# Linear attention with a token-mixing MLP on one core: W_tok loaded and transposed first, its row sums as extra columns, k^T v of two batches in 64x64 tiles

## Chip, core and metric

One core of a Trainium2 chip runs one launch. The metric is the device time of that launch in microseconds. The engines are TensorE (PE), VectorE (DVE), ScalarE (ACT), GpSimd (POOL) and the sync engine SP; SP and POOL issue the DMAs.

## What is computed

Eight batches, eight heads, 576 tokens, head width 64, so 512 features; all inputs and the output are float32.

```python
kv  = einsum('bhsd,bhse->bhde', k, v)
out = einsum('bhsd,bhde->bhse', q, kv)
x   = out / sqrt(mean(out * out, -1) + 1e-6) * g_norm      # heads side by side: (8, 576, 512)
a1  = alpha1 * x + beta1
u   = x + lam * einsum('ts,bsd->btd', w_tok, a1)           # w_tok is 576 x 576
a2  = alpha2 * u + beta2
y   = u + lam * (maximum(a2 @ w_ch1, 0) @ w_ch2)           # 512 -> 2048 -> 512
```

## The kernel before

The program is a list of operations. Each has an engine, operands and a cost that the author set; `schedule` (a planner that runs when the kernel is built) turns the list into one fixed order for each engine and for the DMA issues of SP and POOL. At run time every engine goes through its order and waits at semaphores. PE's operations are in two lists: `main` holds the FFN, `ch1` (L1002, a2 @ w_ch1, 16 groups of 4 matmuls of 512 columns), `ch1_tail` (L1014) and `ch2` (L1031); `fill` holds the rest, which the planner weaves between matmuls of `main`. Where PE would have nothing in the head, fillers are put in (`idler`, matmuls of a tile of ones, L597). `P.shift` and `P.gate` are tables by operation number: the first moves an operation's place in the order, the second lets a DMA wait for another operation.

A batch goes through these steps. `kv` (L749, L755) makes k^T v from k and v as they lie in `kr` and `vr`: rows of 4 tokens, 1024 bytes, by `load_kv` (L1186) and the last 64 tokens apart (L1190); 16 matmuls of 128x128 and 4 for the tail. q is brought to `qt`, transposed: in batches 2 to 7 by DVE (`qt_steady`, L1196, L1199) from rows of 128 bytes (`load_q`, L1178), in batches 0 and 1 by PE (`qt_early`, L703), after a copy on POOL (L698). `norm` (L843, 5 chunks of 4 matmuls) makes q times kv, and ACT (square L807, root L813) and DVE (L810 to L825) the normalized x in `xm` and, times the row e1 = alpha1 * lam * 8 * g_norm, `rm`. `tok` (L914) and `tok_tail` (L948) multiply with the transposed W_tok in `wt`; x is added by DVE (L921). `a2_dma` makes a2 on POOL (L986, L989) and transposes it by DMA (L993) to `a2m`, from which `ch1` starts. `finish` (L1058, L1063) multiplies with lam, adds u, and the output goes out.

Batches 0 and 1 are special. Batch 0's q, k and v come as twelve pieces of two heads each (four of q, of k and of v; 128 partitions with rows of 9 tokens, 2304 bytes; `load_pair`, L611), and its steps are done in halves of four heads: `kv_first` (L725) takes 64x64 matmuls, two row tiles in turn (heads 2p and 2p+1), first for one pair and then for the next; `norm_half` (L864) and `tok_half` (L929) make the norm and the token mix of half the features, with products on POOL (L831, L833), and `a2_pair` (L968, L972) transposes a2 on PE. The row e1 and g are made from four small loads on one partition (L655 to L664) and spread to 128 partitions by a matmul with a row of ones (`e1_rows`, L678, L681).

W_tok (576 x 576) is needed transposed, in bf16, and beta1 is put into the token mix as an extra row of the contraction: `wt`'s last block holds 64 token rows and, at the partitions 64 and 96 for even batches, the sums over s of W_tok, split in a bf16 part and the rest. `rtl`'s rows there hold lam * beta1 (L671). Before, W_tok is loaded after batch 0's q, k and v (L629, one DMA of 1152 KB, and L631), 25 transposes (L1081, L1084) go into `wt` by ACT (L1087, L1092), and `wsums` makes the sums from the finished `wt`: ten matmuls with a matrix `pick` (L1103, L1105), two copies on ACT (L1110) and two subtractions on DVE (L1113). A copy for odd batches follows by DMA (L1118).

The loads of batch 1 are `load_kv(1)` on POOL's queue, after batch 0's last v, and its q on SP's, as pieces of two heads; W1 (L1163) and W2 (L1169) come on POOL's queue in three and two DMAs, converted from float32.

Of the kernel before, what the change touches and what calls it, by code (L numbers as in the profile page):

```python
# [14 lines left out]
NB = 8  # L15
# [38 lines left out]
class Prog:  # L54
    ENGINES = ("PE", "ACT", "DVE", "POOL")

    def __init__(self, nc, stack):
        self.nc, self.stack = nc, stack
        self.ops, self.lastw, self.readers = [], {}, {}
        self.ps = stack.enter_context(nc.psum_tensor("ps", [128, 8, 512], F32))  # L60
        self.eng = {"PE": nc.tensor, "ACT": nc.scalar, "DVE": nc.vector,
                    "POOL": nc.gpsimd, "SP": nc.sync}
        self.spares = 0
        self.pools = {"main": (0, 1, 2, 3), "fill": (4, 5, 6, 7), "any": tuple(range(1, 8))}
        self.main, self.fill = [], []
# [4 lines left out]
        self.gate = {}  # L70

# [36 lines left out]
    def op(self, q, cost, fn, r=(), w=(), pri=0.0, lat=0.15, after=()):  # L108
        o = Op(q, "c", cost, lat, [fn], self.bias + pri, len(self.ops))
        o.bias = self.bias  # L110
        return self._add(o, r, w, after)
# [8 lines left out]
    def mm(self, stream, cols, fns, r=(), w=(), slow=False, after=(), margin=0.3,  # L120
# [8 lines left out]
        o.bias = self.bias  # L129
        o.margin, o.narrow, o.urgent = 0.0 if urgent else margin, cols < 512, urgent  # L130
# [4 lines left out]
    def schedule(self):  # L135
# [26 lines left out]
        for o in self.ops:  # L162
# [4 lines left out]
            elif o.pri - o.bias > -900:  # L167
                o.pri = 1e4 + o.pri
        self.fill.sort(key=lambda o: o.pri)
# [10 lines left out]
        rings = {e: deque() for e in ("SP", "POOL", "ACT")}  # L180
        t, left = 0.0, len(self.ops)
# [38 lines left out]
        def take(o, t, cost=None):  # L220
# [7 lines left out]
            if o.kind == "d":  # L228
                rings[o.q].append([o, t + (1.9 if o.q == "POOL" else 1.1), o.nbytes, False, o.ns,
# [59 lines left out]
        while left:  # L289
# [3 lines left out]
            while moved:  # L293
# [17 lines left out]
                if free["PE"] <= t + 1e-9:  # L311
# [20 lines left out]
                    elif f is not None:  # L332
# [4 lines left out]
                        if f.kind == "w" and not self.began:  # L337
                            g = [o for o in fill[:self.reach] if o.kind == "m" and can(o, t)]
                            if g:
# [3 lines left out]
                                f.end = t + c + f.lat  # L343
# [84 lines left out]
    def woven(f, m):  # L428
# [3 lines left out]
        while i < n or j < k:  # L432
            if i < n and (j >= k or i * k <= j * n):
# [67 lines left out]
def bass_transnormer_attn__then__resmlp_affine_kernel(  # L501
# [15 lines left out]
    with ExitStack() as stack:  # L517
# [6 lines left out]
        pick = sb("pick", [128, 128], BF16)  # L524
# [39 lines left out]
        def nine(flat):  # L564
# [3 lines left out]
        sv = nine(qs[:, 0:2304])  # L568
        hf = hh[:].bitcast(F32)
        wl = hf[:, 0:2304].rearrange("p (c s) -> p c s", c=4)  # L570
        wlt = hf[0:64, 2304:2880]
        qi = [[x.rearrange("p (c f) -> p c f", c=9) for x in y] for y in (
            (hf[:, 2880:4032], tmp[:].rearrange("p i f -> p (i f)")[:, 0:1152]),
# [21 lines left out]
        P.bias = -1000.0  # L595
# [10 lines left out]
        lo, up = slice(0, 64), slice(64, 128)  # L606

        def load_pair(b, n, x, dst, p, after=()):


            P.dma("SP", "%s%d_%d" % (n, b, p), dcost(128, 92), lambda e: e.dma_start(  # L611
# [4 lines left out]
        def load_half(p):  # L616
            for n, x, dst, pp in (("q", q, q0s, (p, p + 1)), ("k", k, k0s, (p,)),
                                  ("v", v, sv, (p,)), ("k", k, k0s, (p + 1,)),
                                  ("v", v, sv, (p + 1,))):
                for i in pp:  # L620
                    load_pair(0, n, x, dst, i)

        load_half(0)
        for i, x, n in ((0, moe_alpha1, DM), (1, moe_lam, DM), (4, g_norm, DH),
                        (2, moe_beta1, DM)):
            P.dma("SP", "row%d" % i, 0.17, lambda e, i=i, x=x, n=n: e.dma_start(
                rows[0:1, i, 0:n], x[None, :]), w=[("row", i)], issue=0.5)
        load_half(2)
        P.dma("SP", "wl", dcost(512, 92), lambda e: e.dma_start(  # L629
            wl, moe_w_tok[0:512, :].rearrange("(c p) s -> p c s", p=128)), w=["wl"])  # L630
        P.dma("SP", "wlt", dcost(64, 220), lambda e: e.dma_start(  # L631
            wlt, moe_w_tok[512:576, :]), w=["wlt"])
        for i, x in enumerate((moe_alpha2, moe_beta2)):
            P.dma("SP", "cst%d" % i, 0.17, lambda e, i=i, x=x: e.dma_start(
# [8 lines left out]
        P.op("DVE", dve(64), lambda e: e.memset(pick[:], 0.0), w=["pick"])  # L643
        P.op("DVE", dve(4), lambda e: e.memset(pick[:, 0:128:32], 1.0), r=["pick"], w=["pick"])
# [9 lines left out]
        P.bias = -500.0  # L654
        y = P.op("DVE", 0.67, lambda e: e.tensor_tensor(  # L655
            out=row(0), in0=row(0), in1=row(1), op=ALU.mult), r=[("row", 0), ("row", 1)],
            w=[("row", 0)])
        x = P.op("DVE", 0.67, lambda e: e.tensor_tensor(
            out=lbrow, in0=row(2), in1=row(1), op=ALU.mult), r=[("row", 1), ("row", 2)],
            w=[("row", 3)])  # L660
        P.op("DVE", 0.2, lambda e: e.tensor_scalar(
            out=row(1, DH), in0=row(4, DH), scalar1=8.0, scalar2=None, op0=ALU.mult),
            r=[("row", 4)], w=[("row", 1)], after=[x, y])
        P.op("DVE", 0.67, lambda e: e.tensor_tensor(  # L664
# [3 lines left out]
            r=[("row", 1), ("row", 0)], w=[("row", 0)])  # L668
        for i, h in ((0, 64), (1, 0)):
# [23 lines left out]
        def qt_early(b, j):  # L693
# [7 lines left out]
            for i in range(3):  # L701
# [4 lines left out]
                    r=["ident", ("qi", b, j, 0), ("qi", b, j, 1)], w=[t], slow=True, urgent=True)  # L706
# [12 lines left out]
        def kv_first(j):  # L719


            ts = [P.bank("any") for _ in range(2)]
            for m in range(2):
                p = 2 * j + m
                P.mm("fill", 64, [lambda e, c=c, s=s, t=t, m=m, p=p: e.matmul(  # L725
                    t.ap(slice(64 * m, 64 * m + 64))[:, 0:64],
                    k0s[64 * s:64 * s + 64, p, c, :], sv[64 * s:64 * s + 64, p, c, :],
                    start=(c == 0), stop=(c == 8), tile_position=(64 * s, 64 * m))
                    for c in range(9) for s, t in enumerate(ts)],
                    r=[("st", "k", p), ("st", "v", p)], w=ts, slow=0.09, urgent=True)  # L730
            for s, t in enumerate(ts):
                for m, rs in enumerate((lo, up)):
                    dst, src = kvc[rs, 0, 2 * j + s, 64 * m:64 * m + 64], lambda t=t, rs=rs: t.ap(
                        rs)[:, 0:64]
                    if s:
                        P.op("DVE", dve(64), lambda e, dst=dst, src=src: e.tensor_copy(
                            out=dst, in_=src()), r=[t], w=[("kv%d" % m, 0, 2 * j + s)], pri=-20)
                    else:
                        P.op("ACT", act(64), lambda e, dst=dst, src=src: e.activation(
                            dst, src(), ACT.Identity), r=[t], w=[("kv%d" % m, 0, 2 * j + s)],  # L740
# [52 lines left out]
        def norm_ops(rs, n, t, xks, rks, dest, shape, flat=None, by="DVE"):  # L793
# [24 lines left out]
            if flat is None:  # L818
# [15 lines left out]
                out=x, in0=x, in1=gv, op=ALU.mult), r=xks + ["g"], w=xks)  # L834
# [19 lines left out]
        def norm_half(j, ch):  # L854
# [18 lines left out]
            if ch == 2:  # L873
# [22 lines left out]
                     "DVE" if j else "POOL")  # L896
# [8 lines left out]
        def wk(b, sc):  # L905
            return [("wt", sc), ("wtt", sc)] if sc < 4 else [("wt", tw(b)), ("wtt", 4), ("ws", tw(b))]
# [69 lines left out]
        def a2_dma(b, c):  # L976
# [3 lines left out]
            else:  # L980
# [5 lines left out]
            P.op("POOL", pool(512), lambda e: e.tensor_tensor(  # L986
# [5 lines left out]
            landing[b] = [P.dma(  # L992
                "SP", "t%d" % c, 0.7, lambda e: e.dma_start_transpose(dst, a2b[:, c]),  # L993
                r=[("a2b", c)], w=dk, issue=0.6)]

# [79 lines left out]
        wtt = P.bank("any")  # L1075

        def wt_group(sc):
            t = P.bank("any")
            n = 128 if sc < 4 else 64
            cols = slice(128 * sc, 128 * sc + n)  # L1080
            P.mm("fill", 128, [lambda e, tc=tc: e.transpose(  # L1081
                t.ap(slice(0, n))[:, 128 * tc:128 * tc + 128], wl[:, tc, cols], ident[:])
                for tc in range(4)], r=["ident", "wl"], w=[t], slow=True)
            P.mm("fill", 64, [lambda e: e.transpose(  # L1084
                wtt.ap(slice(0, n))[:, 64 * sc:64 * sc + 64], wlt[:, cols], ident[0:64, 0:64])],
                r=["ident", "wlt"], w=[wtt], slow=True)
            P.op("ACT", act(512), lambda e: e.activation(  # L1087
                wt[0:n, sc, 0:512], t.ap(slice(0, n)), ACT.Identity), r=[t], w=[("wt", sc)])

        def wt_tail():  # L1090
            for a, z, n in ((0, 4, 128), (4, 5, 64)):
                P.op("ACT", act(64 * (z - a)), lambda e, a=a, z=z, n=n: e.activation(  # L1092
                    wt[0:n, a:z, 512:576],
                    wtt.ap(slice(0, n))[:, 64 * a:64 * z].rearrange("p (c t) -> p c t", t=64),
                    ACT.Identity), r=[wtt], w=[("wtt", i) for i in range(a, z)])

        def wsums():


            for a, z in ((0, 512), (512, 576)):  # L1100
                t = P.bank("any")
                n = z - a
                P.mm("fill", n, [lambda e, sc=sc, t=t, a=a, z=z, n=n: e.matmul(  # L1103
                    t.ap()[:, 0:n], pick[:, :], wt[:, sc, a:z], start=(sc == 0), stop=False)
                    for sc in range(4)] + [lambda e, t=t, a=a, z=z, n=n: e.matmul(  # L1105
                        t.ap()[:, 0:n], pick[0:64, :], wt[0:64, 4, a:z], start=False,
                        stop=True)],
                    r=["pick"] + [(k, i) for k in ("wt", "wtt") for i in range(5)], w=[t])
                for i, h in ((4, 64),):
                    P.op("ACT", act(n), lambda e, i=i, h=h, t=t, a=a, z=z, n=n: e.activation(  # L1110
                        wt[h:h + 64, i, a:z], t.ap(slice(h, h + 64))[:, 0:n], ACT.Identity),
                        r=[t, ("ws", i)], w=[("ws", i)])
                    P.op("DVE", dve(n), lambda e, i=i, h=h, t=t, a=a, z=z, n=n: e.tensor_tensor(  # L1113
                        out=wt[h + 32:h + 64, i, a:z],
                        in0=t.ap(slice(h + 32, h + 64))[:, 0:n], in1=wt[h + 32:h + 64, i, a:z],
                        op=ALU.subtract), r=[t, ("ws", i)], w=[("ws", i)])
            for a, z, key in ((0, 64, ("ws", 5)), (64, 0, ("wt", 5))):
                P.dma("SP", "wt%d" % z, (0.3, 70.0), lambda e, a=a, z=z: e.dma_start(  # L1118
                    wt[a:a + 64, 5, :], wt[z:z + 64, 4, :]), r=[("wt", 4), ("wtt", 4), ("ws", 4)],
                    w=[key])  # L1120

        gate = ()
        for j in range(2):
# [210 lines left out]
```

## Time and profile before

| | |
|---|---|
| time, median of 3 runs | 355.2 us (354.76 to 356.05) |
| profiled execution | 356.56 us, of which 354.8 us are its span |
| PE busy in the span | 341.3 us (96%), 2208 matmul records |
| DVE, ACT, POOL busy | 189.8, 149.0, 161.4 us |
| W_tok's load, issue to landing | 8.3 us |
| first token mix of batch 0 (L929) | 36.54 us |
| first FFN matmul (L1002) | 44.37 us |
| DMA | 48.76 MB, mean 137 GB/s |

The profile is one execution; its times count from the start of the span. Busy time of an engine doesn't tell whether its work was useful: PE's 341.3 us hold 20.0 us of fillers (L597). A line of a group reads: line, engine, operation, output<-input, shapes, count, busy us, mean ns of one, idle us of the engine just before them and what ended it. A float32 matmul that isn't of the kind fp32r appears as two records where it takes two passes.

### The profile page before, as it was taken

How to read it: one execution, taken by the hardware profiler on the slowest of the kernel's cores; microseconds unless marked ns; L12 is line 12 of the kernel's file. 1: busy time of each engine (PE TensorE's matmuls, PEld its weight loads, DVE VectorE, ACT ScalarE, POOL GpSimd, SP SyncE). 2: the span in 40 equal slices, each digit the busy share in tenths (PEclk: the TensorE clock that was granted, in tenths of full speed). 3: DMA queues.
4: the chain of work that ended last, by engine and by line, in shares of the span. 5: the costliest groups of instructions: out<-in, count | busy, mean ns of one | idle time of the engine just before them, and what ended most of it. 6: DMA issues, size and time to landing. Idle time of an engine off the chain costs nothing.

```text
span 354.8 us, 5512 instructions
## 1 busy us (share of the span) xinstructions
PE 341.3 (96%) x2208; PEld 198.4 (56%) x2241; DVE 189.8 (54%) x343; ACT 149.0 (42%) x291; POOL 161.4 (45%) x151
## 2 busy tenths in 40 slices
PE   4979999999999999999999999999999999999994
PEld 3858964454664664466556545564476444444644
DVE  3475778204685579636745676459444963210043
ACT  3335397004940386126823366136552273026400
POOL 2397410965308940985058612973192306930000
PEclk9989999999999999999999999999999999999999
DMA  7999899969598399138963995239922110330012
GB/s 241 267 336 161 139 251 230 144 110 198 120 262 134 90 232 213 31 93 195 247 61 76 221 173 124 46 116 258 175 33 89 59 31 15 75 105 0 2 69 79
DMA packets 107952, 48.76 MB, mean 137 GB/s; under 512 B 81997, under 2 KB 99925, under 8 KB 107928
## 3 DMA queue, kind: packets, MB, share of 16 engines
q1 hardware_dynamic: 82312, 27.71, 42.9%
q0 software_dynamic: 25616, 20.71, 34.0%
q8 instruction: 17, 0.28, 0.3%
q14 instruction: 7, 0.06, 0.1%
HBM read 38.82 MB, written 9.44 MB: 136 GB/s over the span
## 4 chain that ended last, share of the span: by engine, by line
PE 87%; DMA 5%; SPq 2%; POOL 2%; DVE 1%; issue 1%; ACT 0%; DVEq 0%; POOLq 0%
PE ps L1031 31%; PE ps L1002 31%; PE ps L914 8%; PE ps L1014 4%; PE ps L843 3%; DMA hh<-in_moe_w_tok_dram 2%; PE ps L749 2%; DMA w<-in_k_dram 2%; PE ps L597 1%; SPq L611 1%; PE ps L929 1%; POOL a1f L986 1%; PE ps L948 1%; PE ps L1081 1%; PE ps L1042 1%; DMA lam_bc<-in_moe_lam_dram 1%
## 5 line engine op out<-in xcount | busy, mean ns | idle before, releaser
L1031 PE MATMUL ps<-w,hh 128*128 128x512 bf16 x543 | 135.3, 383 | 0.7 <-issue 0.3
L1002 PE MATMUL ps<-a2m,w 128*128 128x512 bf16 x501 | 117.8, 381 | 1.0 <-DVE tmp L1058 0.4
L997 ACT ACTIVATE hh<-ps 128x512 bf16<-128x512 f32 x144 | 84.8, 597 | 64.3 <-PE ps L1002 54.9
L1031 PEld LDWEIGHTS ps<-w,hh 128*128 128x128 bf16 x560 | 52.9, 97 | 58.8 <-issue 1.6
L1002 PEld LDWEIGHTS ps<-a2m,w 128*128 128x128 bf16 x512 | 48.7, 98 | 56.5 <-DVE tmp L1058 1.3
L986 POOL TENSOR_TENSOR a1f<-xm,a_bc 128x512 f32<-128x512 f32 x28 | 35.5, 1273 | 68.6 <-DVE xm L921 68.3
L1058 DVE TENSOR_TENSOR tmp<-ps,lam_bc 128x512 f32<-128x512 f32 (+2 forms) x38 | 25.1, 661 | 69.8 <-PE ps L1031 56.5
L1063 POOL TENSOR_TENSOR xm<-xm,tmp 128x512 f32<-128x512 f32 x28 | 35.4, 1269 | 34.7 <-DVE tmp L1058 34.7
L810 DVE TENSOR_REDUCE small<-sq 128x8 f32<-128x512 f32 (+2 forms) x41 | 27.2, 666 | 25.2 <-ACT sq L807 25.0
L989 POOL TENSOR_TENSOR a2b<-a1f,b_bc 128x512 bf16<-128x512 f32 x32 | 40.3, 1273 | 0.7
L843 PE MATMUL ps<-kvc,qt 128*128 128x128 f32 x140 | 40.1, 395 | 0.0
L921 DVE TENSOR_TENSOR xm<-ps,xm 128x512 f32<-128x512 f32 x28 | 19.3, 690 | 29.8 <-PE ps L914 28.5
L749 PE MATMUL ps<-vr,kr 128*128 128x128 f32 x112 | 32.3, 395 | 0.0
L807 ACT ACTIVATE sq<-ps 128x512 f32<-128x512 f32 (+2 forms) x41 | 23.9, 584 | 19.3 <-PE ps L843 18.5
L1199 ACT ACTIVATE qt<-qp 128x576 fp32r<-128x576 f32 x24 | 15.9, 682 | 32.3 <-DVE qp L1196 32.3
L843 PEld LDWEIGHTS ps<-kvc,qt 128*128 128x128 f32 x140 | 27.4, 199 | 2.0
L914 PE MATMUL ps<-rm,wt 128*128 128x512 bf16 x109 | 28.3, 379 | 0.2
L597 PE MATMUL ps<-fil 128*128 128x128 bf16 x109 | 20.0, 245 | 4.5 <-DVE fil L596 4.5
L819 DVE TENSOR_TENSOR ps<-ps,small 128x512 f32<-128x512 f32 (+1 forms) x35 | 23.5, 690 | 0.5
L766 ACT ACTIVATE kvo<-ps 64x256 f32<-64x256 f32 x14 | 5.3, 378 | 43.0 <-PE ps L755 42.8
L749 PEld LDWEIGHTS ps<-vr,kr 128*128 128x128 f32 x112 | 22.3, 201 | 0.9
L1196 DVE STREAM_TRANSPOSE qp<-qs 128x576 f32<-128x576 f32 x24 | 17.3, 755 | 5.6 <-DMA qs<-in_q_dram 3.4
(109 smaller groups left out, 324.0 us busy)
## 6 DMA issues: line engine op xcount, KB each, us to landing
out_dram<-xm SPq DMA_DIRECT2D x32, 256.0 KB, 2.3
kr<-in_k_dram POOLq DMA_DIRECT2D x7, 1024.0 KB, 9.0
vr<-in_v_dram POOLq DMA_DIRECT2D x7, 1024.0 KB, 11.4
qs<-in_q_dram SPq DMA_DIRECT2D x24, 288.0 KB, 11.1
w<-in_moe_w_ch_dram POOLq DMA_DIRECT2D x3, 1024.0 KB, 10.2
xm<-in_q_dram SPq DMA_DIRECT2D x8, 288.0 KB, 4.4
w<-in_k_dram SPq DMA_DIRECT2D x4, 288.0 KB, 5.6
qs<-in_v_dram SPq DMA_DIRECT2D x4, 288.0 KB, 5.9
```

The lines of the kernel that those rows point to most:

```text
L749: P.mm("fill", 128, [lambda e, t=t, c=c, h=h, o=128 * (h % 4): e.matmul(t.ap()[:, o:o + 128], kr4[:, h, c:c + 2, :].rearrange("p c d -> p ...
L807: P.op("ACT", act(n), lambda e: e.activation(sq[rs, s3, 0:nst, :].rearrange("p h e -> p (h e)"), ps(), ACT.Square), r=[t], w=[("sq", s3)])
L810: P.op("DVE", dve(n), lambda e: e.tensor_reduce(out=st, in_=sq[rs, s3, 0:nst, :], axis=AX.X, op=ALU.add), r=[("sq", s3)], w=[("sm", s4)])
L843: P.mm("fill", 128, [lambda e, p=p: e.matmul(dst(p), qt[:, p, cs], kvc[:, i, p, :], start=(p == 0), stop=(p == 3)) for p in range(4)], r=[ ...
L914: P.mm("fill", 512, [lambda e, sc=sc: e.matmul(t.ap(), wt[:, sc if sc < 4 else tw(b), 128 * c:128 * c + 128], rsrc(b, sc, al), start=(sc = ...
L986: P.op("POOL", pool(512), lambda e: e.tensor_tensor(out=a1f[:, s], in0=x, in1=a2_bc[:], op=ALU.mult), r=ks + ["a2"], w=[("a1f", s)])
L989: P.op("POOL", pool(512), lambda e: e.tensor_tensor(out=a2b[:, c], in0=a1f[:, s], in1=b2_bc[:], op=ALU.add), r=[("a1f", s), "b2"], w=[("a2 ...
L997: P.op("ACT", act(512), lambda e: e.activation(dst, t.ap(), ACT.Relu), r=[t], w=keys, pri=-1000)
L1002: P.mm("main", 512, [lambda e, dj=dj: e.matmul(t.ap(), w1[:, dj, 128 * fj:128 * fj + 128], a2m[:, b % 3, dj, :], start=(dj == 0), stop=(dj ...
L1031: P.mm("main", 512, [lambda e, fj=fj, t=t, c=c: e.matmul(t.ap(), (ht[:, fj, 128 * c:128 * c + 128] if c < 4 else hl[:, fj, :]), w2[:, fj, ...
L1058: P.op("DVE", dve(z - a), lambda e: e.tensor_tensor(out=tmp[:, s, a:z], in0=t.ap()[:, 0:z - a], in1=lam_bc[:, a:z], op=ALU.mult), r=[t, "l ...
L1063: lambda e: e.tensor_tensor(out=x, in0=x, in1=tmp[:, s, a:z], op=ALU.add),
```

## The change

W_tok is loaded first: five DMAs of 128 (the last 64) rows, ahead of batch 0's q, k and v. Each is transposed when it lands, four transposes to a group. W_tok's tile has 64 more columns, set to zero by POOL; DVE sums each row (`tensor_reduce`), writes the sum's bf16 value into column 576 and the rest into column 608, and the last 128 columns, with the sums among them, are transposed as the fifth block. `pick` and `wsums` are gone, and the copy for the odd batches stays.

`kv_first` takes two pairs in one group: four 64x64 tiles in turn (two row tiles, two column tiles). It is also used for batch 1, in place of `kv(1)`; batch 1's k and v are loaded on SP's queue in rows of 2304 bytes, in two halves each, into the places of batch 0's q and v. Batch 2's k is loaded after W2's second half, its v and q after batch 1's transposed tiles have landed (before: v when W1 had been issued, q from 72 us on).

The four products of the constant rows go from DVE to POOL. In batch 0 the product with e1 stays on DVE only for the second half's second chunk and tail. The first product of `a2_dma` (alpha2) goes from POOL to DVE for batch 1. Batch 1's q transposes are no longer `urgent`, so that they can be woven into the FFN. The planner got a `rank` for the head's order, other costs, and new tables `shift` and `gate`, so the order changes everywhere; from batch 2 on, the operations are the same.

```diff
-        load_half(0)
...
-        P.dma("SP", "wl", dcost(512, 92), lambda e: e.dma_start(
-            wl, moe_w_tok[0:512, :].rearrange("(c p) s -> p c s", p=128)), w=["wl"])
-        P.dma("SP", "wlt", dcost(64, 220), lambda e: e.dma_start(
-            wlt, moe_w_tok[512:576, :]), w=["wlt"])
+        for tc in range(4):
+            P.dma("SP", "wl%d" % tc, dcost(128, 100), lambda e, tc=tc: e.dma_start(
+                wl[:, tc, 0:576], moe_w_tok[128 * tc:128 * tc + 128, :]), w=[("wl", tc)])
+        P.dma("SP", "wlt", dcost(64, 200), lambda e: e.dma_start(
+            wlt[:, 0:576], moe_w_tok[512:576, :]), w=[("wl", 4)])
+        for p in range(2):
+            load_pair(0, "q", q, q0s, p)
...
-        def kv_first(j):
+        def kv_first(b, j):
...
+            ps = (j, j + 2) if b else (2 * j, 2 * j + 1)
+            P.mm("fill", 64, [lambda e, c=c, s=s, t=t, m=m, p=p: e.matmul(
+                t.ap(slice(64 * m, 64 * m + 64))[:, 0:64],
+                ks[64 * s:64 * s + 64, p, c, :], vs[64 * s:64 * s + 64, p, c, :],
+                start=(c == 0), stop=(c == 8), tile_position=(64 * s, 64 * m))
+                for c in range(9) for m, p in enumerate(ps) for s, t in enumerate(ts)],
...
-                     "DVE" if j else "POOL")
+                     "DVE" if j and ch else "POOL")
...
+            first = b == 1
+            P.op("DVE" if first else "POOL", dve(512) if first else pool(512),
+                 lambda e: e.tensor_tensor(
                 out=a1f[:, s], in0=x, in1=a2_bc[:], op=ALU.mult), r=ks + ["a2"],
                 w=[("a1f", s)])
...
+        def wt_sum(tc):
+            n = 128 if tc < 4 else 64
+            src = wl[:, tc, :] if tc < 4 else wlt
+            P.op("DVE", dve(576), lambda e: e.tensor_reduce(
+                out=wsv[0:n, tc:tc + 1], in_=src[:, 0:576], axis=AX.X, op=ALU.add),
+                r=[("wl", tc)], w=[("wsv", tc)])
+            P.op("DVE", 0.17, lambda e: e.tensor_copy(
+                out=wsh[0:n, tc:tc + 1], in_=wsv[0:n, tc:tc + 1]), r=[("wsv", tc)],
+                w=[("wsh", tc)])
+            P.op("DVE", 0.17, lambda e: e.tensor_copy(
+                out=src[:, 576:577], in_=wsh[0:n, tc:tc + 1]),
+                r=[("wsh", tc)], w=[("pad", tc if tc == 4 else 0)])
+            P.op("DVE", 0.17, lambda e: e.tensor_tensor(
+                out=src[:, 608:609], in0=wsv[0:n, tc:tc + 1], in1=wsh[0:n, tc:tc + 1],
+                op=ALU.subtract), r=[("wsv", tc), ("wsh", tc)], w=[("pad", tc if tc == 4 else 0)])
...
+        for n, x, t in (("k", k, k1s), ("v", v, v1s)):
+            for j in range(2):
+                P.dma("SP", "%s1%d" % (n, j), dcost(256, 100), lambda e, x=x, t=t, j=j: e.dma_start(
+                    t[:, j::2].rearrange("p i c d -> p i (c d)"),
+                    x[1].rearrange("(i h) (g c) d -> (h g) i (c d)", h=2, c=9)[:, j::2]),
+                    w=[("st", n + "1", j), ("st", n + "1", j + 2)], after=k3)
...
-        load_kv(1, v3)
...
-            load_w2(i, 2, [P.lastw[("v", 0)][0]], 1 + i)
+            load_w2(i, 2, [P.lastw[("st", "v1", 0)][0]], 1 + i)
...
+            if b == 1:
+                load_kv(2, [P.lastw[("w2", 2)][0]], "k")
+            elif b + 1 < NB:
+                load_kv(b + 1, landing[b - 1])
+                load_q(b + 1, landing[b - 1])
...
+            if b == 1:
+                P.bias = 100.0 * b
+                load_kv(2, landing[1], "v")
+                load_q(2, landing[1])
...
-        P.t0 = -470.9
-        P.pace = 3.102
+        P.t0 = -122.8
+        P.pace = 1.054
```

More of the change, by code (lines that the diff above doesn't have):

```diff
@@ L180, in schedule @@
         rings = {e: deque() for e in ("SP", "POOL", "ACT")}
+        begun = {}
         t, left = 0.0, len(self.ops)
@@ L228, in take @@
             if o.kind == "d":
-                rings[o.q].append([o, t + (1.9 if o.q == "POOL" else 1.1), o.nbytes, False, o.ns,
+                begun[o.q] = begun.get(o.q, 0) + 1
+                extra = 0.85 if o.q == "SP" and begun[o.q] == 3 else 0.0
+                rings[o.q].append([o, t + (1.9 if o.q == "POOL" else 1.1), o.nbytes + extra,
+                                   False, o.ns,
                                    o.slot[0] == "t"])
@@ L905, in wk @@
         def wk(b, sc):
-            return [("wt", sc), ("wtt", sc)] if sc < 4 else [("wt", tw(b)), ("wtt", 4), ("ws", tw(b))]
+            return [("wt", i) for i in range(5)] if sc < 4 else (
+                [("wtt", 0), ("wtt", 1)] if b % 2 == 0 else [("ws", 5), ("wu", 5)])
         def lb(i):
@@ L1072, in finish @@
                           r=ks[len(pp) * i:len(pp) * i + len(pp)])
[L1075 to L1117, printed above, removed]
@@ new lines, in wt_group @@
+        def wt_group(tc):
+            t, n = P.bank("any"), 128 if tc < 4 else 64
+            src = wl[:, tc, :] if tc < 4 else wlt
+            P.mm("fill", 128, [lambda e, sc=sc: e.transpose(
+                t.ap()[:, n * sc:n * sc + n], src[:, 128 * sc:128 * sc + 128],
+                ident[0:n, 0:n]) for sc in range(4)], r=["ident", ("wl", tc)], w=[t], slow=True)
+            P.op("ACT", act(4 * n), lambda e: e.activation(
+                wt[:, 0:4, 128 * tc:128 * tc + n],
+                t.ap()[:, 0:4 * n].rearrange("p (c t) -> p c t", c=4), ACT.Identity),
+                r=[t], w=[("wt", tc)])
@@ L1182, in load_q, with load_kv @@
                     after=after)
-        def load_kv(b, after=()):
+        def load_kv(b, after=(), which="kv"):
             for n, x, m, tl in (("k", k, kr4, krt), ("v", v, vr4, vrt)):
+                if n not in which:
+                    continue
                 P.dma("POOL", n + "r", dcost(1024, 72), lambda e, x=x, m=m: e.dma_start(
@@ L1233, in attention @@
                         t[64:128, 2048:2560].bitcast(F32), 0.0), w=[n + "z"])
-            kv(b)
-            if b == 1:
+            if b > 1:
+                kv(b)
+                for p in range(4):
+                    qt_steady(p)
+            else:
+                for j in range(2):
+                    kv_first(1, j)
+                alias([("x", i, c, p) for i in (1, 2) for c in range(4) for p in range(4)],
+                      st("k1"))
+                alias([("qs", g) for g in range(4)], st("v1"))
                 for j in range(2):
```

150 lines of the change are left out of this document (89 added, 61 removed), and 28 rows, old and new, of the table cs.

## Prediction

> **What bounds the kernel now.** I read the page first: TensorE (PE) is busy for 341.3 of 354.8 us, but its 40 slices and the clock row show that the first 30 us differ from the rest.
>
> ```profile
> PE   4979999999999999999999999999999999999994
> PEclk9989999999999999999999999999999999999999
> ```
>
> Then the chain of waits in order of time, for the places where the chain changes its carrier:
>
> ```profile
> 15.58 8.33 DMA hh<-in_moe_w_tok_dram
> 23.95 0.33 PE ps L1081
> 31.73 0.81 PE ps L1103 x3
> 36.70 1.09 PE ps L929 x10
> 44.37 0.38 PE ps L1002
> 52.74 7.93 PE ps L1002 x36
> 350.36 0.30 DVE tmp L1058
> ```
>
> To 23.95 us the end hangs on the load of W_tok. Its transposes (L1081), the row sums (L1103), batch 0's token mix (L929) and its transposes follow; at 44.37 the first FFN matmul (L1002) starts. From there to 350.36 PE has 306.0 us of back-to-back work: its steps add up to 305.0 (1,212 matmuls of 512 columns at 0.216, 256 of L1014 at 0.056, 256 float32 ones in the FFN's shadow at 0.075, the tails and 8 transposes 9.7), so only 1 us of it is waiting. So two things decide: when the first FFN matmul can start, and how much PE work is still left then.
>
> **What the head is made of.** The timeline of GpSimd (POOL) gives landings, because it waits for them:
>
> ```profile
> 3.67 0.66 POOL L698 COPY hh<-xm 128x576 f32<-128x576 f32 x1 [2.21 <-DMA xm<-in_q_dram]
> 11.77 0.67 POOL L698 COPY tmp<-xm 128x576 f32<-128x576 f32 x1 [0.41 <-DMA xm<-in_q_dram]
> 16.27 1.07 POOL L1186 DMA_DIRECT2D kr<-in_k_dram  x1 [3.83 <-DMA qs<-in_v_dram]
> ```
>
> These are the 1st, the 8th and the last (12th) of batch 0's 295 KB pieces of q, k and v. The stretches of 2.5 us give the rate meanwhile (last column GB/s):
>
> ```profile
> 2.50:5.00 2.50, 0.48 (x5) 0.49 (x6) 1.77 (x7) 0.00 (x0) 0.88 (x2) 1.00 0.95 302
> 5.00:7.50 2.50, 2.50 (x19) 1.89 (x17) 0.00 (x0) 0.53 (x1) 0.45 (x1) 1.00 0.96 309
> 7.50:10.00 2.50, 2.22 (x29) 1.78 (x29) 0.00 (x0) 1.08 (x3) 0.00 (x0) 1.00 1.03 351
> 10.00:12.50 2.50, 2.19 (x58) 1.97 (x55) 0.25 (x2) 0.25 (x2) 1.33 (x2) 1.00 1.00 298
> ```
>
> **The change, part by part.** 1. W_tok first. Its 1.33 MB are 4.5 more pieces ahead of q, k and v, so the last v is piece 16.5. At 1.16 us a piece (3.67 to 11.77 in 7 steps) it lands at 3.67 + 15.5 x 1.16 = 21.7; at the mean 315 GB/s of the four stretches, 4.87 MB take 15.5 us from 2.5, plus about 1 to land: 19.0. I take 20.0, nearer to the rate, since the first steps hold the start of the queue. Cost to the loads: about 4 us. In return the 25 transposes, the five row reductions and 15 small DVE operations lie under loading: PE idled and ran fillers there, and DVE waited 7.75 us for L725. They cost nothing while v is still on its way. Removed are the sums' ten matmuls, their evictions and the stretch from 31.73 to 36.5 in which the token mix waited for them.
>
> 2. What is late next is the row e1 and GpSimd. From the order of the changed program: last v, then 36 matmuls of 64x64 (the four-tile form), the broadcast matmul of e1, its copy on ACT, and on GpSimd two products with e1, one with g, and the tail's product, before PE's token mix of the first half may start. Rows:
>
> ```profile
> L831 POOL TENSOR_TENSOR rm<-xm,e_bc 128x512 bf16<-128x512 f32 x2 | 2.5, 1266 | 0.0
> L833 POOL TENSOR_TENSOR xm<-xm,g_bc 128x512 f32<-128x512 f32 x4 | 5.4, 1354 | 0.8 <-DVE rm L831 0.7
> L831 POOL TENSOR_TENSOR rtl<-xt,e_bc 64x256 bf16<-64x256 f32 x1 | 0.7, 716 | 0.7 <-ACT e_bc L681 0.7
> L948 PE MATMUL ps<-rm,wt 128*64 128x512 bf16 x32 | 4.2, 385 | 0.0
> ```
>
> e1 took 1.16 us on PE (20.87 to the copy at 22.03) and 0.60 on ACT. GpSimd now also makes the four rows of constants, three at 1.27 to 1.35 and one at 0.3; begun when their loads land, near 16, they end near 20.5, inside the wait for v and its matmuls. So: 20.0 + 1.2 (v's matmuls) + 1.2 + 0.7 + (1.27 + 1.27 + 1.35 + 0.72 = 4.6) + 0.4 of hops = 28.1 for the token mix, where it was 36.5.
>
> 3. From there to the first FFN matmul PE has 20 steps of the token mix (0.109 each, 2.2), 4 transposes and 36 four-tile matmuls (1.6), 20 more steps and 8 transposes (28 x 0.109 = 3.1) and again 36 four-tile matmuls (1.2): 28.1 + 8.1 = 36.2. GpSimd's product for the second half (after one more product with g 1.35, a copy 0.67, then 1.27) is done near 31.4, before PE asks for it at 31.9. With 0.6 for hops and copies: 36.8 instead of 44.37, 7.6 us earlier.
>
> 4. The four-tile price. L725 ran two tiles at a time:
>
> ```profile
> 10.93 1.26 PE L725 MATMUL ps<-qs,w 64*64 64x64 f32 x36
> ```
>
> Those are 18 matmuls in two passes each: two row tiles start 7 ns apart, the next two 58 ns later, 1.05 us in all. If two column tiles overlap as well, 36 matmuls take the same, with the starts 1.2; if not, 2.1. L948 is the nearest row: its two column tiles overlap (8 matmuls of 512 columns in 1.05 us, where 8 at 0.216 make 1.7). I take 1.2 and keep 2.1 for the range; the group stands on the path three times. The Trainium skill ("TensorE: Matmul & The Clock Gate", Packing small matmuls) says that a weight load overlaps matmuls in flight only where the row group differs; two column tiles share their row group. By that rule each group would take the 2.1, and the time would be 353.3.
>
> 5. Work left at the first FFN matmul. Before, batch 1's k^T v (20 matmuls), its 18 q transposes and 4 of its norm matmuls were done by 44.37. After, k^T v is done too, but 14 transposes and 4 norm matmuls come later: 14 x 0.109 + 4 x 0.075 = 1.8, and 19 norm matmuls now follow one another instead of an FFN matmul (0.11 against 0.075): 0.7. So PE ends 2.5 us later than the start alone says.
>
> 6. Moved loads and new waits. Batch 1's k and v now take SP's queue in two halves each, beside W1's first quarter: 3.25 + 1.05 MB from 20.0 at the stretches' 298 to 351 GB/s end at 32.3 to 34.4; PE asks for the last half at 35.5. So hidden by little; up to 1 us if not. W1's rest and W2 leave GpSimd in one row from 33: at 6.0 us per 2.1 MB (W2's first half landed 6.0 after the load ahead of it in before) they land near 39, 45, 51 and 57 and are needed near 45, 49, 55 and 67. GpSimd then waits for W2's second half before batch 2's k, and behind that stand batch 1's five a2b products (from 62): clear by 5 us. The products with alpha2 for batch 1 go to DVE, 5 x 0.69 where it is busy for 4.1 of 20 us; GpSimd loses 5 x 1.27 there and the 0.4 us stall at 81.4, behind the late load of lam, goes with it. Batch 2's v and q wait for batch 1's transposes (near 68.5), and are needed near 82 and 86: rival 3. For all of these I allow 0.5 us.
>
> **Sum.** 7.6 - 2.5 - 0.5 = 4.6 us. Span 354.8 - 4.6 = 350.2. The profiled execution took 356.56, 1.8 outside its span; the runs' median is 355.2, so 355.2 - 4.6 = 350.6.
>
> **The rivals.** 1. Column tiles don't overlap: three groups of 2.1 instead of 1.2 make 2.7 us, so 353.3. For it: weights of 64 float32 columns are reloaded for each matmul; against it: L948. Chance 0.13. (The Trainium skill's rule under 4 would give this case.)
>
> 2. The loads, not the arithmetic, set the new head: v lands at 21.7, and batch 1's halves 1 us after PE asks. 1.7 + 1.0 = 2.7, so 353.3; half of it 352. For it: the step of 1.16 us; against it: 351 GB/s at 7.5 to 10. Chance 0.15.
>
> 3. Slower: batch 2's v and q come too late. Before, its v left at 40.55 and its q from 72; now both leave when batch 1's last full tile has been transposed. The first transposed tile of before landed 6.9 us after its issue beside a W2 load, not 2.4; and behind kr and vr a q piece took 15.4. The waits that decide: PE's first k^T v matmul of batch 2, and DVE's transposes of q, whose four take 3.7 us with ACT's copies before the norm matmuls that PE reaches near 90. With tiles at 68.5 + 4.5 = 73, q issued to 75 and landed at 91, PE waits until 95: 5 us, 355.6; a second late round for batch 3 makes 358. It decides from a q that lands after 86. For it: 4 us of slack only, on loads that were spread over 45 us before; against it: kr is already in, so less stands in the queue. Chance 0.11, of which 0.07 with the second round.
>
> **How the numbers follow.** Forecast 0.61: from 349.2 (v at 19.0 and no stray waits, 1.4 less) to 352.4 (1.8 more, the unknowns at their dear end). The range, 349.0 to 354.6, adds rivals 1 and 2, and some overlap of the two; rival 3 and the far ends are left out. A measurement of this kernel tells about 0.5%, 1.8 us, from no change, so faster means below 353.4 and slower above 357.0. Faster: the forecast's 0.61, half of rival 1 (0.065) and two thirds of rival 2 (0.10), 0.78. Slower: rival 3 with its second round, 0.07. Within: the rest of the three, 0.15.
>
> **What would show it.** Right: the first FFN matmul (L1027 of the changed kernel) at 35.4 to 38.5, the first token mix at 27 to 30, released by GpSimd; 36 four-tile matmuls in about 1.2 to 1.4 us; PE then without waits over 0.5 us. Wrong: groups of 2.1 us (rival 1); the four-tile group of batch 0's second half released by v after 21.5, or those of batch 1 by DMA (rival 2); PE idle before batch 2's k^T v or norm matmuls, between 80 and 96 (rival 3); or a first FFN matmul after 41, which no row above accounts for.

## The result, and the profile after

The changed kernel took 358.37 us (median of 4 runs, 357.90 to 358.61) beside 355.61 us for the kernel before (354.76 to 356.05): a ratio of 1.0079, 95% interval 1.0055 to 1.0103. It is slower by 0.8%, where I had forecast 350.6 us and 4.6 us of gain. The profiled execution took 358.44 us, with a span of 356.6 us.

The chain that ended last, for the changed kernel, in order of time (start, us, what; L1027 is the first FFN layer, L1039 its tail for odd batches, L744 the four-tile k^T v, L950 batch 0's token mix):

```profile
0.74 2.89 DMA hh<-in_moe_w_tok_dram
...
20.28 1.21 PE ps L744 x72
...
27.94 2.18 PE ps L950 x20
30.23 0.26 PE ps L744 x2
30.49 0.26 PE ps L721
...
37.50 0.38 PE ps L1027
...
75.20 7.50 PE ps L1027 x34
...
87.40 0.61 ACT hh L1022
...
88.02 8.08 DMA a2l<-a2b
...
96.14 6.29 PE ps L1039 x64
```

The head did what it should: W_tok's load is 2.9 us of the chain instead of 8.3, and the first FFN matmul starts at 37.50 us, 6.9 us earlier than the 44.37 of before. But from there to the end of the span it takes 356.6 - 37.5 = 319.1 us, where the kernel before took 354.8 - 44.37 = 310.4. So 8.7 us were given back behind the head, and the chain shows where to look: at 87.40 it leaves TensorE, over a ReLU for a DMA.

The page's slices, of 8.9 us each:

```profile
PE   7999999999599999999999999999999999999995
PEclk9999999999889999999999999999999999999999
```

TensorE is half busy in the eleventh slice (89 to 98 us), and in that and the next one the granted clock is down. TensorE's timeline there (start, busy us, line, shapes, count, and in brackets the idle time before and what ended it):

```profile
92.14 2.00 PE L863 MATMUL ps<-kvc,qt 128*128 128x128 f32 x16 [1.88 <-ACT qt L1233]
96.14 6.29 PE L1039 MATMUL ps<-a2l,w 128*128 128x128 bf16 x64 [2.01 <-DMA a2l<-a2b]
```

Two gaps, one before the normalisation of batch 2, one before the 64 small matmuls of batch 1's tail. In the kernel before these matmuls (L1014 there) came without a wait:

```profile
96.97 3.74 PE L1014 MATMUL ps<-a2l,w 128*128 128x128 bf16 x64
```

They took 3.74 us there (3.57 as the chain counts it); here 6.29. The stretches show why (third column from the right: granted clock):

```profile
94.00:96.00 2.00, 0.14 (x2) 0.00 (x0) 1.82 (x6) 1.65 (x6) 0.00 (x0) 0.67 1.86 383
96.00:98.00 2.00, 1.85 (x18) 1.86 (x19) 2.00 (x4) 0.13 (x1) 0.00 (x0) 0.50 2.02 256
...
100.00:102.00 2.00, 2.00 (x26) 2.00 (x25) 0.00 (x0) 0.89 (x2) 0.00 (x0) 0.62 1.02 152
```

The clock is 0.50 from about 94.7 to 101.5 us (a mean of 0.67 over 2 us is 1.3 us at half speed, one of 0.62 is 1.5). So the rows offer 1.9 + 2.0 us of waiting and 2.5 to 2.7 us of slow matmuls, and the 2.5 us of work that I had moved behind the first FFN matmul: about 9, against 8.7.

**Where the waits come from.** a2l, the transposed a2 of batch 1's last 64 tokens, took 8.08 us; in the kernel before it took 2.43 (91.04 to 93.47; issues of 84 to 112 us, last column: us from issue to landing):

```profile
a2l<-a2b SPq DMA_TRANSPOSE x1, 2.4
```

What differs is a line of the diff that I had read past:

```diff
-            landing[b] = [P.dma(
+            d = [P.dma(
                 "SP", "t%d" % c, 0.7, lambda e: e.dma_start_transpose(dst, a2b[:, c]),
                 r=[("a2b", c)], w=dk, issue=0.6)]
+            if c < 4:
+                landing[b] = d
```

`landing[b - 1]` is what the loads of batch b + 1 wait for. Before, for batch 3, that was a2l itself; now it is the transpose of chunk 3. So GpSimd issues batch 3's k at 87.43 and its v at 88.34, around a2l, which `P.gate` (295: 474) holds back to 88.02, behind batch 1's thirteenth ReLU. Its operand was ready at 71.87. That from batch 2 on the operations are the same, as I wrote of the change, is true of the operations, but not of what their loads wait for.

The other wait is one of order, not of data. Batch 2's q landed at 82.68, VectorE had two of its four transposes done at 84.14, and ScalarE, which copies them, had them behind the fourteenth of batch 1's sixteen ReLUs:

```profile
88.26 0.60 ACT L1022 ACTIVATE hh<-ps 128x512 bf16<-128x512 f32 x1 [0.27 <-PE ps L1027]
88.75 1.25 ACT L1233 ACTIVATE qt<-qp 128x576 fp32r<-128x576 f32 x2
```

VectorE's other two transposes waited for these copies (5.32 us, until 89.46).

### The profile page after: what moved, and what is told of

It reads as the page before. It is cut to its first block, busy times and chain, and to the rows that moved or that the text cites. A ratio compares the mean times of both kernels' runs of the same rounds, so it can differ in the third digit from the quotient of the medians.

```text
span 356.6 us, 5946 instructions
## 1 busy us (share of the span) xinstructions
PE 344.4 (97%) x2411; PEld 202.3 (57%) x2444; DVE 194.8 (55%) x361; ACT 148.4 (42%) x291; POOL 157.4 (44%) x149
## 4 chain that ended last, share of the span: by engine, by line
PE 95%; DMA 3%; issue 1%; ACT 0%; DVE 0%
PE ps L1056 34%; PE ps L1027 30%; PE ps L935 8%; PE ps L1039 5%; PE ps L611 3%; PE ps L863 2%; DMA a2l<-a2b 2%; PE ps L769 2%; PE ps L744 2%; PE ps L969 1%; PE ps L721 1%; PE ps L950 1%; PE ps L1067 1%; PE ps L1105 1%; DMA hh<-in_moe_w_tok_dram 1%; PE ps L884 1%
## 5 line engine op out<-in xcount | busy, mean ns | idle before, releaser
L1056 PE MATMUL ps<-w,hh 128*128 128x512 bf16 x545 | 133.3, 382 | 0.8 <-issue 0.2
L1027 PE MATMUL ps<-a2m,w 128*128 128x512 bf16 x499 | 119.2, 381 | 0.6 <-issue 0.2
L1027 PEld LDWEIGHTS ps<-a2m,w 128*128 128x128 bf16 x512 | 48.9, 98 | 55.1
L1009 POOL TENSOR_TENSOR a1f<-xm,a_bc 128x512 f32<-128x512 f32 x24 | 30.4, 1270 | 61.7 <-DVE xm L942 61.4
L863 PE MATMUL ps<-kvc,qt 128*128 128x128 f32 x140 | 36.9, 380 | 1.9 <-ACT qt L1233 1.9
L769 PE MATMUL ps<-vr,kr 128*128 128x128 f32 x96 | 28.8, 408 | 0.0
L863 PEld LDWEIGHTS ps<-kvc,qt 128*128 128x128 f32 x140 | 25.5, 198 | 4.1 <-ACT qt L1233 2.4
L611 PE MATMUL ps<-fil 128*128 128x128 bf16 x198 | 21.0, 230 | 2.1 <-DVE fil L610 2.1
L1039 PE MATMUL ps<-a2l,w 128*128 128x128 bf16 x256 | 18.2, 238 | 2.1 <-DMA a2l<-a2b 2.0
L769 PEld LDWEIGHTS ps<-vr,kr 128*128 128x128 f32 x96 | 19.2, 200 | 0.8
```

Source lines behind the costliest of these rows:

```text
L611: P.spare_fn = lambda e: e.matmul(P.ps[:, 0, 0:128], fil[:], fil[:], start=True, stop=True)
L769: P.mm("fill", 128, [lambda e, t=t, c=c, h=h, o=128 * (h % 4): e.matmul(t.ap()[:, o:o + 128], kr4[:, h, c:c + 2, :].rearrange("p c d -> p ...
L863: P.mm("fill", 128, [lambda e, p=p: e.matmul(dst(p), qt[:, p, cs], kvc[:, i, p, :], start=(p == 0), stop=(p == 3)) for p in range(4)], r=[ ...
L1009: lambda e: e.tensor_tensor(out=a1f[:, s], in0=x, in1=a2_bc[:], op=ALU.mult), r=ks + ["a2"],
L1027: P.mm("main", 512, [lambda e, dj=dj: e.matmul(t.ap(), w1[:, dj, 128 * fj:128 * fj + 128], a2m[:, b % 3, dj, :], start=(dj == 0), stop=(dj ...
L1039: P.mm("main", 128, [lambda e, dj=dj, fj=fj: e.matmul(t.ap()[:, 128 * fj:128 * fj + 128], w1[:, dj, 128 * (f4 + fj):128 * (f4 + fj) + 128] ...
```

## The experiments

My theory: the head's gain is there, and batch 2 loses it to these two waits and to the clock behind them. The rival: the loss is spread over the run (more work on TensorE, busier queues), and the two gaps are its symptom. All edits are made behind `P.schedule()`, so that TensorE's order stays as it is; `move(i, j)` puts operation i behind operation j in the list from which each engine takes its order. Operations: 295 is the transpose to a2l, 474 the thirteenth ReLU, 363 batch 0's last store, 381 to 384 batch 3's k and v, 385 to 388 its q, 373 to 380 batch 2's transposes and copies of q.

**1. The transpose earlier.**

```diff
+        P.ops[295].deps.discard(P.ops[474])
+        move(295, 363)
```

> The changed kernel, with the transpose of batch 1's tail (a2l) no longer held behind batch 1's thirteenth ReLU: SyncE issues it behind batch 0's four stores, at about 83 instead of 88.02 us, ahead of batch 3's k, v and q. Every engine's order stays. Theory: TensorE lost 1.9 us before the normalisation of batch 2 (q's copies on ScalarE), 2.0 us on a2l (8.1 us in flight beside batch 3's loads), and 2.7 us because the clock was 0.50 afterwards. a2l lands by 86 us, the 2.0 us are gone; if the clock falls only where both gaps come together, the 64 small matmuls take 3.6 us again: 358.4 - 2.0 - 2.7 = 353.7 us. Rival A, the clock falls from the first gap alone: 356.4 us. Rival B, the loss is not in this place (work and loads spread over the run): 358.4 us.

355.04 us (354.21 to 358.05, 10 runs; before in the same rounds 356.11), ratio 0.9971 (0.9938 to 1.0004). a2l was issued at 83.24 and landed at 87.48, later than the 86 that I expected, and TensorE did not wait for it. Five runs are at 354.2 to 354.9 us with a mean clock of 0.998 or 0.999, three at 355.2 to 355.9 with 0.994 or 0.995, two at 358.0 with 0.990: the gap of 1.88 us that is left lowers the clock in some runs and not in others. A mean clock 0.009 lower is 6.4 us at half speed in 353, worth up to 3.2 us, about the distance of the last group from the first.

**2. The loads behind the transpose, as before.**

```diff
+        for i in range(381, 389):
+            P.ops[i].deps.add(P.ops[295])
+        move(381, 295)
```

> The changed kernel, with batch 3's loads of k, v and q waiting for a2l, as the kernel before had it; a2l is issued at 88.0 us as in the changed kernel. Every engine's order stays. Theory (the transpose took 8.1 us because of the loads beside it): it lands after 2.4 us, at 90.4 to 91, no wait for it on TensorE, 353.7 us if the clock stays up, 356.4 if the first gap alone lowers it. Rival, the transpose is slow whatever is beside it: lands at 96 and 358.4 us, or more, since batch 3's loads come 8 us later. Batch 3's k and v start 3 us later in the first case, and are needed near 107: no cost expected.

354.41 us (353.85 to 357.97, 10 runs), ratio 0.9988 (0.9944 to 1.0031); again in groups, seven runs at 353.9 to 354.7 (clock 0.998 or 0.999) and three at 357.9 (0.990). The transpose was issued at 87.97, as in the changed kernel. The DMA issues of 84 to 112 us, in the changed kernel and in this one:

```profile
a2l<-a2b SPq DMA_TRANSPOSE x1, 8.1
```

```profile
a2l<-a2b SPq DMA_TRANSPOSE x1, 2.5
```

TensorE's timeline of this kernel: the first gap is unchanged, the second gone, the 64 matmuls fast.

```profile
92.09 2.00 PE L863 MATMUL ps<-kvc,qt 128*128 128x128 f32 x16 [1.88 <-ACT qt L1233]
93.93 3.75 PE L1039 MATMUL ps<-a2l,w 128*128 128x128 bf16 x64
```

So it was neither the size nor the time of the transpose but its company, and batch 3's loads bear a start 3 us later without cost.

**3. Which load.** Experiment 2 for 381 to 384 alone, and for 385 to 388 alone.

> The changed kernel, where only batch 3's k and v (GpSimd's queue) wait for a2l; its q (SyncE's queue, issued some 2.9 us behind a2l) is free. Theory, k and v slow the transpose: a2l, issued at 88.0, lands at 90.4 to 91.5, no wait for it, most runs near 354.4 us as where all loads waited. Rival, q's many small packets slow it: lands after 94, 357 to 358.4 us.

> The opposite: only batch 3's q waits for a2l, its k and v are issued at 87.4 and 88.3 us as in the changed kernel. Theory, k and v slow the transpose: it lands near 96, TensorE waits 2 us, 358.4 us. Rival, q does: lands by 92, near 354.4 us.

With k and v held back the transpose took 2.48 us and the median was 354.41 us (10 runs; ratio 0.9983, 0.9942 to 1.0024); with q held back, 8.01 us and 358.58 us (10 runs; ratio 1.0086, 1.0049 to 1.0124). TensorE waited 0.68 us for it there, not the 2 us that I expected: in that profile the clock had fallen after the first gap already, and the normalisation ahead of the tail took 3.25 us instead of 2.00. k and v on GpSimd's queue are enough to slow it. What q alone would do isn't shown: it is issued after a2l has landed.

**4. ScalarE's order alone.** The copies of q go one by one between the last ReLUs:

```diff
+        for i, j in ((373, 363), (375, 373), (374, 468), (376, 470), (377, 376),
+                     (379, 377), (378, 472), (380, 474)):
+            move(i, j)
```

> The changed kernel, with ScalarE's four copies of batch 2's q placed between batch 1's last ReLUs instead of behind them (and VectorE's transposes of it ahead of them); q itself landed at 82.7 us and is not loaded sooner. Theory: the gap of 1.9 us before the normalisation of batch 2 goes or shrinks to some 0.2, but TensorE then waits that much longer for a2l, which still lands at 96.1 or later: a gap of 3.5 to 4 us in one piece, clock low behind it, 358.4 us, within 1 us. Rival, the two waits add up independently: 356.5 us.

358.39 us (357.96 to 359.82, 10 runs), ratio 1.0086 (1.0057 to 1.0114): no gain, as the theory has it.

```profile
91.34 1.97 PE L863 MATMUL ps<-kvc,qt 128*128 128x128 f32 x16 [0.36 <-DVE kvc L788]
96.88 5.07 PE L1039 MATMUL ps<-a2l,w 128*128 128x128 bf16 x64 [3.56 <-DMA a2l<-a2b]
```

The first gap shrank by 1.5 us and the second grew by 1.5: TensorE only came to the later wait sooner. The two waits don't add up; the later one ends last.

**5. Both edits** (1 and 4).

> The changed kernel with both edits: a2l at 83 us and q's copies earlier. Theory: no gap over 0.3 us on TensorE between 75 and 105 us, the clock at 1.00 there, 358.4 - 1.9 - 2.0 - 2.7 = 351.8 us, against 355.6 of the kernel before. Rival B (the loss is spread): 358.4. Rival C (another wait follows, for batch 3's loads or the bias tiles): 354 to 355.

352.66 us (352.45 to 352.73, 4 runs), ratio 0.9895 (0.9843 to 0.9948).

```profile
90.99 1.97 PE L863 MATMUL ps<-kvc,qt 128*128 128x128 f32 x16 [0.36 <-DVE kvc L788]
92.81 3.75 PE L1039 MATMUL ps<-a2l,w 128*128 128x128 bf16 x64
```

By the medians this version beats both kernels. It was timed once more, with the changed kernel, in five rounds:

> The mended kernel (the transpose of a2l at 83 us and q's copies earlier) once more, in five rounds beside the changed kernel and the kernel before on one chip. From its first run: 352.7 us, a ratio to the kernel before of 0.990, and a narrow spread, since neither the head nor batch 2 has a gap over 0.4 us after which the clock could fall.

> The changed kernel as it is, in the same rounds: 358.4 us, a ratio to the kernel before of 1.008, so 5.7 us above the mended one. Of these, 1.9 - 0.4 us are the gap before the normalisation, 2.0 us the wait for a2l, and 2.5 us the clock: 6.0 us by the rows.

The mended kernel: 352.76 us (352.26 to 353.38, 12 runs), ratio 0.9930 (0.9908 to 0.9951). The changed one: 358.16 us (357.82 to 359.97, 6 runs), ratio 1.010 (1.0061 to 1.0140). The difference is 5.4 us where the rows gave 6.0.

**6. The clock by itself.** Small matmuls on constant data fill the gaps; every wait stays.

```diff
+            f = Op("PE", "m", 0.0, 0.0, [lambda e: e.matmul(
+                P.ps[:, o.alloc[0].bank, 0:128], fil[:], fil[:], start=True, stop=True)] * n,
+                0.0, -1000 - i)
...
+        fillers(405, ..., 28)     # ahead of batch 2's normalisation
+        fillers(481, ..., 30)     # ahead of the tail's first layer
```

> The changed kernel with all its waits as they are, and small matmuls on constant data put into TensorE's order in the two gaps: 28 (some 1.6 us) ahead of the normalisation of batch 2, 30 (some 1.7 us) ahead of the tail's first layer; nothing reads what they write. They add no useful work and no wait goes away. Theory (the clock falls because TensorE stands idle twice): the clock stays at 1.00, the tail's 64 matmuls still start near 96.1 us and take 3.75 instead of 6.29 us: 358.4 - 2.5 = 355.9 us. Rival, the clock falls for another reason (the load, the float32 matmuls between): 358.4 us.

356.56 us (355.92 to 357.35, 10 runs), ratio 1.0011 (0.9987 to 1.0036), with a mean clock of 0.997 to 1.00 in every run. The tail still has to wait for a2l, but runs at full speed:

```profile
96.92 3.75 PE L1039 MATMUL ps<-a2l,w 128*128 128x128 bf16 x64 [0.34 <-DMA a2l<-a2b]
```

So idleness lowered the clock, and the clock's share is 2.5 us by the row (6.29 - 3.75) and 1.6 to 1.8 by the medians. With the first gap alone filled:

> As the run with both gaps filled, but only the first gap (ahead of the normalisation) is filled; the 2.0 us on a2l stay idle. If it takes both gaps close together to lower the clock in every run, most runs are at 355.9 us and a few at 358 to 359 (one gap of 1.9 us alone gave 354.2 to 355.9 us in 7 of 10 runs and 358.0 in 3, in the run with the early transpose). If the second gap alone does it: 358.4 in all.

358.08 us (355.82 to 358.71, 10 runs), ratio 1.0041 (1.0021 to 1.0061): eight runs at 357.7 to 358.7, and two at 355.8 and 356.6 with the clock at 0.999 and 1.00. I had expected the reverse proportion; it doesn't take both gaps. (The 7 and 3 that the expectation quotes are those of experiment 2; with the early transpose it was 8 and 2.)

```profile
96.29 6.29 PE L1039 MATMUL ps<-a2l,w 128*128 128x128 bf16 x64 [2.05 <-DMA a2l<-a2b]
```

**7. The same fault put into the kernel before.** Its batch 3 loads (368 to 375) no longer wait for a2l (282).

```diff
+        for i in range(368, 376):
+            P.ops[i].deps.discard(P.ops[282])
```

> The kernel before, where batch 3's loads of k and v no longer wait for a2l; every engine's order stays. GpSimd then issues them from about 86.7 us instead of 93.8, ahead of a2l (91.04). Theory (the transpose is slow beside those loads): a2l lands at 98 to 99 instead of 93.5 us, the tail's first layer, which began at 96.97 us, waits 1 to 2 us for it: the kernel before plus 1 to 2 us, or plus 4 to 5 where the clock falls too. Rival, the order of the loads does not matter: a2l lands by 94, no change.

Four runs: 355.61 us (the profiled one, mean clock 0.995) and 361.05 to 362.41 with 0.986; they are too far apart for a ratio, and the first lies within the 353.3 to 357.7 us of the kernel before in these rounds. So these times don't show a price. The profile shows the mechanism: the transpose again took 8.0 us, and the tail (L1014 here) waited and ran slowly.

```profile
94.39 5.36 PE L1014 MATMUL ps<-a2l,w 128*128 128x128 bf16 x64 [1.90 <-DMA a2l<-a2b]
```

By the rows that is 1.90 us of waiting and 1.6 us of slow matmuls (5.36 instead of 3.74). They don't appear in this run's time because its head was early: the first FFN matmul started at 39.88 us, not at 44.37 as in the profile before, and the edit has no part in that (see the last section). Why the other three runs take 361 to 362 us is not shown.

**8. The four tiles taken back,** in the mended kernel.

```diff
-                for c in range(9) for m, p in enumerate(ps) for s, t in enumerate(ts)],
+                for m, p in enumerate(ps) for c in range(9) for s, t in enumerate(ts)],
```

> The mended kernel (both edits), with each group of 36 k^T v matmuls of batches 0 and 1 issued as 18 of one pair of 64x64 tiles and then 18 of the other, instead of the four in turn: the same matmuls, no other change. By the rows of the kernel before, 18 in two tiles took 1.05 us, so a group takes 2.1 instead of 1.28 us. All four groups lie on TensorE's path by my reading (the second one of batch 0 directly, the first while k and v still land): 352.7 + 2 x 0.82 for batch 1 + 0.82 for the last group of batch 0 = 355.1 us. Rival, the groups are covered by waits for loads and products: 352.7 to 353.5 us.

356.23 us (355.59 to 356.99, 10 runs), ratio 1.0009 (0.9988 to 1.0030): 3.5 us slower than the mended kernel and 1.1 more than I expected, so all four groups lie on TensorE's path, the first one too. TensorE's timelines, the mended kernel and this one (72 records are 36 matmuls in two passes):

```profile
20.59 1.28 PE L744 MATMUL ps<-qs,w 64*64 64x64 f32 x72
```

```profile
21.30 2.14 PE L744 MATMUL ps<-qs,w 64*64 64x64 f32 x72
```

The order of the loop is worth 0.86 us a group, four times; without it even the mended kernel is no faster than the one before.

## Why the prediction was wrong, step by step

- **1, W_tok's loading (v at 20.0):** v landed at 17.53; 4.87 MB by then is a better rate than I took. It made no difference: TensorE, with its transposes, normalisation and the fillers woven between them, came to v's matmuls at 20.21.
- **2, the chain to the token mix (28.1):** 27.78, behind GpSimd's products as described.
- **3, the first FFN matmul (36.8):** 37.50, and 37.87 in the mended kernel's first run. The term that was too small is batch 1's first group: its first six records alternate with q transposes, at about 0.26 us for each pair of records and as much for each transpose (the lines at 30.23 and 30.49), so that stretch took 2.74 us, not 1.6.
- **4, the four-tile price (1.2, or 2.1 as rival 1):** 1.21 in the chain. Rival 1 is out. But the groups stand on the path four times, by experiment 8, and not three: rival 1 would have cost the 3.5 us of experiment 8, not 2.7. The Trainium skill's rule ("TensorE: Matmul & The Clock Gate", Packing small matmuls), by which a group would take 2.1 us since two column tiles share a row group, isn't what this case shows: 1.21 us with the four tiles in turn.
- **5, the work left (+2.5):** in the mended kernel the first FFN matmul to the span's end is 350.8 - 37.87 = 312.9 us, 2.5 more than before. Right.
- **6, moved loads and new waits (0.5):** this is the step that failed. It cost some 6 us in the changed kernel, and next to nothing in the mended one. I followed the loads that the change moves by name (batch 2's), and not those that it frees by a changed dependency (batch 3's): a2l has no place in my text at all. The price stood in my own text: under rival 3 a transposed tile lands 6.9 us after its issue beside a W2 load, not 2.4. I also said that TensorE would be without waits over 0.5 us, on the strength of landing times, without working out the order in which ScalarE would take q's copies.
- **Rival 3** had the place (TensorE idle before batch 2's normalisation, between 80 and 96) but not the mechanism: it was to decide from a q that lands after 86, and q landed at 82.68. Its price, 355.6 to 358, came near by accident. No rival held a price for the clock, which more than doubled what the second wait cost; the dip in the third slice of PEclk in my first view, behind the wait for W_tok, could have warned me.
- **The sum:** I forecast a span of 350.2 us, and it was 356.6. Of the 6.4 us, 0.7 are step 3 and 5.7 step 6 (8.7 given back, less the 2.5 of step 5 and the 0.5 allowed). The other 1.4 between 350.6 and 358.4 come of taking the steps from a profiled execution of 356.56 us and subtracting their sum from the median of 355.2. With step 6 mended the profiled execution goes from 356.56 to 352.66, 3.9 us instead of 4.6.

## What to carry to other kernels

Where a change edits what a transfer waits for, list every transfer that becomes free earlier, and what small, urgent transfer will then stand beside it. Price a gap on TensorE with the clock: here 2.0 us of waiting brought 2.5 us of slow matmuls with it. And take away all waits of a stage together before judging one of them: the edit to ScalarE's order was worth nothing alone and 2 us behind the other. And ask of a wait in a profile whether other executions have it: the head that I set out to shorten was 4.5 us shorter in another trace of the same head.

## What the runs showed of the hardware

- **A DMA transpose beside bulk loads.** The same 64-token transpose of batch 1 took 2.4 to 2.5 us alone (three kernels), 4.2 to 4.7 behind the four 256 KB stores of the same queue, and 8.0 to 8.2 beside k and v of 1 MB each on GpSimd's queue (six kernels).
- **The clock can fall from a gap of 1.9 to 2.05 us.** By the mean clock of the runs (0.995 or less; it tells that the clock fell, and only the profiled runs show where), it fell in 12 of 30 runs with the gap of 1.88 us alone (experiments 1, 2 and 3), in 8 of 10 with the later gap of 2.05 alone, and in all 10 runs of the changed kernel, which has both. It also fell in all 10 with the one gap of 3.56 us (experiment 4). The fall isn't tied to the end of a gap: in the changed kernel it fell 0.5 us into the second one, and in the run with k and v held back 1.7 us after the end of the only one (at 93.9, from its stretches). Why the two single gaps differ is open. The Trainium skill ("TensorE: Matmul & The Clock Gate", Why this matters for your kernels) sets the limit at gaps of about 3 us; here 1.9 us were enough at times.
- **It stays low in steps of 3.4 us:** 6.8 us here (94.7 to 101.5), 6.8 with the first gap filled, 3.4 in experiments 4 and 7. The Trainium skill ("TensorE: Matmul & The Clock Gate", Part 1) describes a free-running window of about 3.4 us, and these traces agree with that length.
- **The kernel before has such a gap in its head, and not in every run.** In its profile TensorE waits 1.96 us for W_tok, and the clock falls:

```profile
23.95 0.33 PE L1081 MATMUL ps<-ident,hh 128*128 128x128 f32 x1 [1.96 <-DMA hh<-in_moe_w_tok_dram]
24.00:26.00 2.00, 2.00 (x14) 1.61 (x15) 1.80 (x2) 0.00 (x0) 1.92 (x2) 0.54 1.65 376
```

  The profile of experiment 7 has the same operations in the head. There W_tok was issued 1.35 us earlier and took 7.0 instead of 8.3 us, the clock stayed at 1.00 from 20 to 32 us, and the first FFN matmul started 4.5 us earlier:

```profile
21.29 0.33 PE L1081 MATMUL ps<-ident,hh 128*128 128x128 f32 x1 [0.41 <-DMA hh<-in_moe_w_tok_dram]
```

  This fits the spread of the kernel before, though no trace shows one of its fastest runs. In the rounds of the experiments 7 of its runs had a mean clock of 0.999 or 1.00, and these took 352.0 to 353.6 us; 77 others, at 0.987 to 0.995, took 353.7 to 358.0. The mended kernel has no gap over 0.4 us after its first matmul in either profile, and its 12 runs in five rounds took 352.3 to 353.4. So it is no faster than the kernel before at its best; it is faster than that kernel's usual run.
